# Two blocks of w_in loaded and converted earlier, two first-layer steps moved to attention steps 34 and 35, and four subtractions given to GpSimd

## The chip, the cores and the metric

One core of one Trainium2 chip runs the whole kernel. The metric is the device time of one execution in microseconds (us). Inputs are laid out on the host before the launch, which is not timed.

## What is computed

Three stages follow one another. Attention over q, k, v (4 batches, 8 heads, 576 positions, 64 dimensions) uses a local mask for four heads and a strided mask for the other four. Its output, 2304 tokens by 512, goes through a dense layer pair and then through a routed one:

```
scores = where(mask, q @ k.T / 8, -1e9); attn = softmax(scores); x = attn @ v
h = x @ w_in                       # w_in is 512 x 2048, float64 bits
x2 = (s * relu(h)**2 + b) @ w_out  # w_out is 2048 x 512
logits = x2 @ w_gate               # 8 experts, 288 tokens each, greedy by logit
out[tokens of e] = relu(x2 @ w1[e]) @ w2[e]
```

The arrays `w_in` and `w_out` arrive as 64-bit words and the kernel itself makes float32 from them.

## The kernel before

The kernel is written by hand in a fixed order: each engine runs its own instructions strictly in the order in which the Python code issues them, and waits on semaphores for its operands. Nothing is reordered at run time, so an instruction that waits holds everything behind it on its engine.

**The attention loop.** `mix1` runs a loop over a counter k, called the attention step here. A unit is one pair of heads and one half of the positions of a batch; units 0 to 15 are the first two batches. Unit u starts at step 2u and advances one phase a step. Its phases, with the engine and the line in the kernel before, are:

- step 2u+2: scores on TensorE (L256, L263)
- step 2u+3: row maximum on VectorE (L279, for strided units also the subtraction L290)
- step 2u+4: exponential on ScalarE (L284 or L292)
- step 2u+6: normalisation on VectorE (L296 to L299)
- step 2u+9: transposes on TensorE (L308 or L310)
- step 2u+10: copy of the transposed tile to SBUF on ScalarE (`eT`, L320)
- step 2u+12: product with v on TensorE (L331)
- step 2u+13: copy into `xb` on ScalarE (L336 or L340)

Once enough units are done, `group_x` makes the operands of a group of 384 tokens: a rounded part `xh` on ScalarE (L373) and the rest `xl` on VectorE (L374).

**Blocks of w_in.** `prep(i)` with even i makes block i/2 of the sixteen column blocks of `w_in`. It loads the raw words (L381), takes their absolute value on ScalarE (L406), converts them with four VectorE instructions (L409 to L412), rounds the result to `wh` on ScalarE (L392) and subtracts, `wl = W - wh`, on VectorE (L394). Blocks 0 and 1 go through the pipe `prep0`, which ticks at every second attention step from `P0S` on and starts one block a tick. The later blocks go through `prep`, which ticks at every second step from `P2S = 30` on. A block waits `CA = 4` ticks between the load and the absolute value if `i < 4`, and two ticks otherwise.

**First-layer steps.** `h_step(g, fc)` multiplies group g by block fc on TensorE with twelve matmuls of 128x384: four `wh`·`xh`, four `wh`·`xl` and four `wl`·`xh` (L500), then applies relu and square on ScalarE (L505, L506) and stores the result (L508). `H0` lists the attention steps at which h_step(0, 0) and h_step(0, 1) stand; all other steps follow after the attention loop, the first two of them being (1, 0) and (0, 2). A step's relu is issued when the next step is.

The rest of the program (second layer, routing, experts) is not touched.

Of the kernel before, what the change touches and what calls it, by code (L numbers as in the profile page):

```python
# [13 lines left out]
ALU = mybir.AluOpType  # L14
# [15 lines left out]
def _f(ap):  # L30
    return ap.bitcast(F32)
# [43 lines left out]
class Body:  # L75
# [12 lines left out]
    F2 = 1024  # L88
    WS = 54
    RW = 7  # L90
    CA = 4
    LATE0 = 30
    FA0 = 13
# [8 lines left out]
    A2S = 8  # L102
    TM = 2
    FE = (4, 14, 20)
    P0S = 20
    P2S = 30
    H0 = (36, 38)
    AE = 2
    LOADLAG = 2
    MANUAL = True  # L110
# [39 lines left out]
    def wide(self, shape, dt, s):  # L150
        return self.w.tile(shape, dt, tag="rw", name=self.nm(s), bufs=self.RW)

# [228 lines left out]
        self.nc.sync.dma_start(t.rearrange("p f t -> p (f t)"), self.a["words"][i // 2, i % 2])  # L381
        return t

    def split(self, W, put, wide=False):
        nc = self.nc
        if wide:
            t = self.wide([128, 2, 512], F32R, "wh")
            h, l = t[:, 0], t[:, 1]
        else:
            h = self.wt([128, 512], F32R, "wh")  # L390
            l = self.wt([128, 512], F32R, "wl")
        nc.scalar.copy(h, W)  # L392
        yield
        nc.vector.tensor_tensor(l, W, _f(h), op=ALU.subtract)  # L394
        put((h, l))

    def prep(self, i):

        nc = self.nc
        fc = i // 2  # L400
        raw = self.conv_load(i)
        for _ in range(self.CA if i < 4 or i % 2 else 2):
            yield
        K = self.wt([128, 512], I32, "K")
        ts = nc.vector.tensor_scalar
        nc.scalar.activation(_f(K), _f(raw[:, :, 1]), AF.Abs)  # L406
        yield
        W = self.wt([128, 512], I32, "W")
        ts(_f(K), _f(K), D64_MIN, D64_MAX, op0=ALU.max, op1=ALU.min)  # L409
        ts(K, K, 3, 0x3FFFFFFF, op0=ALU.logical_shift_left, op1=ALU.bitwise_and)  # L410
        nc.vector.scalar_tensor_tensor(W, raw[:, :, 1], -0x40000000, K, op0=ALU.bitwise_and, op1=ALU.bitwise_or)
        nc.vector.scalar_tensor_tensor(K, raw[:, :, 0], 29, W, op0=ALU.logical_shift_right, op1=ALU.bitwise_or)  # L412
        W = _f(K)
        yield
        if i % 2 == 0:
            yield from self.split(W, lambda v: self.win.__setitem__(fc, v))
            return
        nc.sync.dma_start(self.wod[fc], W)
        yield
        yield  # L420
        ps = self.ps()
        for dc in range(4):
            nc.tensor.transpose(ps[:, dc * 128:(dc + 1) * 128], W[:, dc * 128:(dc + 1) * 128], self.identf)  # L423
        yield
        WT = self.wt([128, 512], F32, "WT")
        nc.scalar.copy(WT, ps)
        yield
        self.WTs.append(WT)
        if len(self.WTs) < 4:
            return  # L430
        ps = self.ps()
        for k, WT in enumerate(self.WTs):
            for dc in range(4):
                sl = slice(dc * 128, (dc + 1) * 128)
                nc.tensor.matmul(ps[32 * dc:32 * dc + 32, k * 128:(k + 1) * 128], self.gate[:, dc, :], WT[:, sl],
                                 start=True, stop=True, skip_group_check=True)
        self.WTs.clear()
        yield
        go = self.wt([128, 512], F32, "go")
        nc.scalar.copy(go, ps)  # L440
        yield
        ps = self.ps()
        for k in range(4):
            nc.tensor.transpose(ps[:, k * 128:(k + 1) * 128], go[:, k * 128:(k + 1) * 128], self.identf)
        yield
        nc.vector.tensor_reduce(self.wog[:, fc * 8 - 24:fc * 8 + 8].rearrange("p (f e) -> p f e", e=8),
                                ps.rearrange("p (f c e) -> p f e c", f=4, c=4)[:, :, :8, :], axis=AX.X, op=ALU.add)
        yield
        self.nwog += 4
        if self.nwog == 16:  # L450
            self.prep_end()
# [12 lines left out]
    def load_out(self, fc):  # L464
# [4 lines left out]
        yield  # L469
        yield from self.split(t, lambda v: self.wout.__setitem__(fc, v), fc < self.RW)  # L470
        if fc == 0:
# [117 lines left out]
    def mix1(self):  # L589
# [23 lines left out]
        self.late_pipe = Pipe(self.late_step(g, fc) for g in range(self.NG) for fc in range(16))  # L613
        lead = len(self.H0)
        seq = [(0, fc) for fc in range(lead)] + [(1 - g, fc + g * lead) for fc in range(12) for g in (0, 1)]
# [5 lines left out]
        while self.units < 14 or not self.win or ready:  # L621
            if k in self.H0:
                assert len(self.xg[0]) == 4
# [7 lines left out]
            if self.KS <= k < self.KE:  # L631
                self.keep_warm(self.KW)
            if k >= self.P0S and k % self.P0R == 0:
                prep0.tick()
# [289 lines left out]
    def prep2(self, e, w1, w2):  # L924
        nc, a = self.nc, self.a

        def one(src, put, wide=False):
            t = self.wt([128, 512], F32, "raw2")
            nc.sync.dma_start(t, src)
            yield  # L930
            yield
            yield from self.split(t, put, wide)
# [5 lines left out]
        for fc in range(8):  # L938
            yield one(a["w2"][e, fc * 128:(fc + 1) * 128, :], lambda v, i=fc: w2.__setitem__(i, v),
                      e % 2 == 1 and fc >= 8 - self.RW)  # L940

# [255 lines left out]
```

## Time and profile before

| | us |
|---|---|
| median of 3 runs | 746.08 |
| lowest and highest of these | 744.84, 748.76 |
| the profiled execution, its own time | 750.04 |
| its span from first to last instruction | 748.3 |
| TensorE busy | 724.6 (97%) |
| VectorE busy | 497.0 (66%) |
| ScalarE busy | 371.2 (50%) |
| GpSimd busy | 58.4 (8%) |

The profiled execution took 3.96 us more than the median of the runs. TensorE is busy nearly throughout, and its mean granted clock is 0.987 of full speed. The busy shares are means over stages with different limits, so the stage of the change has to be read by itself.

### The profile page before, as it was taken

To read this page: it belongs to the slowest core of one execution; us is meant where nothing else is said; L and a number is where in the kernel's file an instruction comes from. 1 tells how busy PE (TensorE), PEld (TensorE's weight loads), DVE (VectorE), ACT (ScalarE), POOL (GpSimd) and SP (SyncE) were. 2 spreads that over 40 slices of the span, in tenths; PEclk is the share of its full clock that TensorE was granted. 3 is DMA by queue.
4 is the path that set the end of the run, shared out by engine and by line. 5 is a ranking of instruction groups with operands and counts; after the bars stand their busy time and mean duration, and the time that the engine had idled before them with its cause. 6 is when DMAs were issued, how large, how long until landed. Compare 5 with 4: busy or idle time off the path is not lost.

```text
span 748.3 us, 16505 instructions
## 1 busy us (share of the span) xinstructions
PE 724.6 (97%) x6276; PEld 647.3 (87%) x6276; DVE 497.0 (66%) x1158; ACT 371.2 (50%) x861; POOL 58.4 (8%) x81
## 2 busy tenths in 40 slices
PE   8989999999999999999999998999999999999996
PEld 6769998999999878788778777877999999999994
DVE  6888999986551344378798887785466666666620
ACT  4878775777666555521414221230355554555520
POOL 4000000000000000000000000001102312321211
PEclk9969999999999999999999999999999999999999
DMA  7946866775785899634444423341766676674511
GB/s 232 292 134 201 280 199 198 244 251 191 267 311 187 259 297 288 192 132 144 153 140 143 158 86 116 95 159 44 222 229 180 194 234 202 224 210 146 194 33 32
DMA packets 80047, 140.17 MB, mean 187 GB/s; under 512 B 10336, under 2 KB 43872, under 8 KB 79968
## 3 DMA queue, kind: packets, MB, share of 16 engines
q1 hardware_dynamic: 76896, 129.68, 53.9%
q0 software_dynamic: 3072, 9.44, 3.7%
q8 instruction: 49, 0.80, 0.4%
q14 instruction: 30, 0.25, 0.1%
HBM read 106.32 MB, written 32.77 MB: 186 GB/s over the span
## 4 chain that ended last, share of the span: by engine, by line
PE 85%; DVE 9%; DMA 3%; issue 2%; ACT 0%; POOLq 0%; SPq 0%; DVEq 0%; ACTq 0%
PE b L500 25%; PE b L732 17%; PE b L1000 13%; PE b L1025 11%; PE b L263 3%; PE b L331 2%; PE b L537 2%; DMA r<-ud 2%; PE b L1063 1%; PE b L954 1%; DVE u L704 1%; PE b L1041 1%; PE b L308 1%; DVE E L554 1%; PE b L423 1%
## 5 line engine op out<-in xcount | busy, mean ns | idle before, releaser
L732 PE MATMUL b<-wh,u 128*128 128x512 f32 x663 | 179.6, 391 | 1.1 <-DVE u L704 1.1
L732 PEld LDWEIGHTS b<-wh,u 128*128 128x128 f32 x663 | 121.5, 192 | 17.8 <-DVE u L704 1.8
L701 ACT CAST u<-r 128x384 fp32r<-128x384 f32 (+1 forms) x96 | 46.2, 493 | 130.3 <-DMA r<-ud 62.0
L1025 PE MATMUL b<-u,wh 128*128 128x288 f32 x532 | 90.5, 293 | 0.0
L500 PE MATMUL b<-xh,wh 128*128 128x384 f32 x384 | 84.6, 344 | 0.0
L500 PE MATMUL b<-xh,wl 128*128 128x384 f32 x384 | 79.8, 331 | 2.1 <-DVE wl L394 2.1
L500 PE MATMUL b<-xl,wh 128*128 128x384 f32 x384 | 79.5, 331 | 0.0
L392 ACT CAST wh<-raw 128x512 fp32r<-128x512 f32 x128 | 73.3, 618 | 10.5 <-DVE u L704 10.4
L505 ACT ACTIVATE r<-b 128x384 f32<-128x384 f32 x96 | 46.9, 489 | 63.2 <-PE b L500 61.4
L1025 PEld LDWEIGHTS b<-u,wh 128*128 128x128 f32 x532 | 75.6, 190 | 0.0
L1000 PE MATMUL b<-X,wh 128*128 128x288 f32 x512 | 73.4, 287 | 0.6 <-ACT X L973 0.6
L500 PEld LDWEIGHTS b<-xh,wh 128*128 128x128 f32 x384 | 63.6, 193 | 7.4 <-PE b L537 3.7
L1000 PEld LDWEIGHTS b<-X,wh 128*128 128x128 f32 x512 | 67.4, 189 | 1.3 <-ACT X L973 0.7
L500 PEld LDWEIGHTS b<-xh,wl 128*128 128x128 f32 x384 | 66.0, 192 | 2.9 <-DVE wl L394 2.9
L1007 DVE SCALAR_TENSOR_TENSOR u<-b,u 128x288 fp32r<-128x288 f32 x64 | 29.2, 456 | 57.7 <-ACT u L1006 57.7
L500 PEld LDWEIGHTS b<-xl,wh 128*128 128x128 f32 x384 | 66.2, 192 | 0.0
L394 DVE TENSOR_TENSOR wl<-raw,wh 128x512 fp32r<-128x512 f32 x100 | 65.0, 683 | 0.3
L704 DVE TENSOR_TENSOR u<-r,u 128x384 fp32r<-128x384 f32 (+1 forms) x96 | 47.9, 527 | 17.0 <-ACT u L701 17.0
L732 PE MATMUL b<-wl,u 128*128 128x512 f32 x153 | 58.2, 381 | 0.0
L506 ACT ACTIVATE r<-r 128x384 f32<-128x384 f32 x96 | 50.5, 526 | 3.0
L1006 ACT ACTIVATE u<-b 128x288 fp32r<-128x288 f32 x64 | 26.3, 411 | 50.5 <-PE b L1000 50.2
L1000 PE MATMUL b<-X,wl 128*128 128x288 f32 x256 | 41.9, 286 | 0.0
(209 smaller groups left out, 1096.6 us busy)
## 6 DMA issues: line engine op xcount, KB each, us to landing
raw<-in_moe_w_dram SPq DMA_DIRECT2D x128, 256.0 KB, 4.4
r<-ud SPq DMA_DIRECT2D x160, 192.0 KB, 4.1
ud<-r SPq DMA_DIRECT2D x96, 192.0 KB, 3.0
raw<-in_words_dram SPq DMA_DIRECT2D x32, 512.0 KB, 4.2
qk<-in_q_dram SPq DMA_DIRECT2D x24, 288.0 KB, 4.0
x2d<-E SPq DMA_DIRECT2D x18, 256.0 KB
wod<-K SPq DMA_DIRECT2D x16, 256.0 KB, 2.5
wo<-wod SPq DMA_DIRECT2D x16, 256.0 KB, 4.7
```

The lines of the kernel that those rows point to most:

```text
L392: nc.scalar.copy(h, W)
L394: nc.vector.tensor_tensor(l, W, _f(h), op=ALU.subtract)
L500: nc.tensor.matmul(ps[:, :self.G], w[:, dc * 128:(dc + 1) * 128], _alt(self.xg[g][dc][x]), start=(k == 0), stop=(k == 11))
L505: nc.scalar.activation(_two(r), _nat(ps[:, :self.G]), AF.Relu)
L506: nc.scalar.activation(r, r, AF.Square)
L701: nc.scalar.copy(d[0], src)
L704: nc.vector.tensor_tensor(d[1], src, _f(d[0]), op=ALU.subtract)
L732: self.nc.tensor.matmul(**args)
L1000: self.nc.tensor.matmul(ps[:, :288], w1[dc, fh][wi][:, fs:fs + 128], _alt(X[:, xi, dc, :]), start=(k == 0), stop=(k == 11))
L1006: self.nc.scalar.activation(_two(h), _nat(ps[:, :288]), AF.Relu)
L1007: self.nc.vector.scalar_tensor_tensor(_two(l), _nat(ps[:, :288]), 0.0, _two(_f(h)), op0=ALU.max, op1=ALU.subtract)
L1025: nc.tensor.matmul(y[dc][:, :288], w[:, sl], _alt(u[:, j, :288]), start=(fc == 0 and i == 0), stop=(fc == 7 and i == 2))
```

## The change

Four things change. Blocks 0 and 1 start at attention step 18 rather than 20 (`P0S`), and they wait two ticks rather than four between load and absolute value, as the other blocks do. The steps h_step(0, 0) and h_step(0, 1) stand at attention steps 34 and 35 rather than 36 and 38 (`H0`). The subtraction `wl` of blocks 0 to 3 is issued on GpSimd (`GL = 4`).

```
+    GL = 4
-    P0S = 20
+    P0S = 18
-    H0 = (36, 38)
+    H0 = (34, 35)

-    def split(self, W, put, wide=False):
+    def split(self, W, put, wide=False, by=None):
...
         nc.scalar.copy(h, W)
         yield
-        nc.vector.tensor_tensor(l, W, _f(h), op=ALU.subtract)
+        (by or nc.vector).tensor_tensor(l, W, _f(h), op=ALU.subtract)
...
-        for _ in range(self.CA if i < 4 or i % 2 else 2):
+        for _ in range(self.CA if i % 2 else 2):
             yield
...
-            yield from self.split(W, lambda v: self.win.__setitem__(fc, v))
+            yield from self.split(W, lambda v: self.win.__setitem__(fc, v), by=nc.gpsimd if fc < self.GL else None)
```

Line numbers of the changed kernel are one higher than those of the kernel before from L91 on.

**VectorE, attention steps 24 to 27.** In the kernel before, the normalisation of unit 9 (`E_131`) is followed by the maximum of unit 11, the normalisation of unit 10 (`E_663`) and the maximum of unit 12:

```order
L299 TENSOR_TENSOR E_131<-E_131,nm_613 100x8x36
L279 TENSOR_REDUCE nm_719<-b_694 100x8
L290 TENSOR_TENSOR E_129<-b_694,nm_719 100x8x36
L297 TENSOR_SCALAR nm_662<-nm_662 128x5
L298 RECIPROCAL nm_662<-nm_662 128x5
L299 TENSOR_TENSOR E_663<-E_663,nm_662 128x480
L279 TENSOR_REDUCE nm_766<-b_742 100x8
```

In the changed kernel the same stretch reads:

```order
L300 TENSOR_TENSOR E_131<-E_131,nm_615 100x8x36
L410 TENSOR_SCALAR K_658<-K_658 128x512
L411 TENSOR_SCALAR K_658<-K_658 128x512
L412 SCALAR_TENSOR_TENSOR W_716<-raw_546,K_658 128x512
L413 SCALAR_TENSOR_TENSOR K_658<-raw_546,W_716 128x512
L280 TENSOR_REDUCE nm_728<-b_696 100x8
L291 TENSOR_TENSOR E_129<-b_696,nm_728 100x8x36
L298 TENSOR_SCALAR nm_664<-nm_664 128x5
L299 RECIPROCAL nm_664<-nm_664 128x5
L300 TENSOR_TENSOR E_665<-E_665,nm_664 128x480
L410 TENSOR_SCALAR K_721<-K_721 128x512
```

The four conversion instructions of block 0 (`K_658`) moved ahead of unit 11's maximum and those of block 1 (`K_721`) ahead of unit 12's; before, they stood six steps later, behind the normalisations of units 12 and 13.

**ScalarE, attention steps 34 to 36.** Here stand, before the change, the exponential of unit 15 (`E_965`), `wh` of block 1, the absolute value of block 2, the copies of unit 11 into `xb` and the `eT` copy of unit 13:

```order
L284 ACTIVATE E_965,nm_964<-b_941,nm_964 128x96 x4
L392 CAST wh_1007<-K_896 128x512
L406 ACTIVATE K_1010<-raw_898 128x512
L340 COPY xb_831<-b_979 128x4x36
L340 COPY xb_831<-b_980 128x4x36
L320 COPY eT_1056<-b_1018 96x384
```

And in the changed kernel:

```order
L285 ACTIVATE E_970,nm_969<-b_954,nm_969 128x96 x4
L407 ACTIVATE K_1024<-raw_911 128x512
L506 ACTIVATE r_1028<-b_984 128x384
L507 ACTIVATE r_1028<-r_1028 128x384
L341 COPY xb_850<-b_997 128x4x36
L341 COPY xb_850<-b_998 128x4x36
L321 COPY eT_1073<-b_1048 96x384
```

The rounding of block 1 left this place for an earlier one, and relu and square of h_step(0, 0) moved ahead of unit 11's and unit 13's copies.

**TensorE, attention steps 34 to 36.** Before, the last matmuls of unit 11's product with v (`eT_932`) and the five transposes of unit 13 (`E_838`) stand ahead of the first matmuls of h_step(0, 0):

```order
L331 MATMUL b_980<-eT_932,v_763 64x36 x2
L308 MATMUL b_1018<-identf,E_838 96x128
L308 MATMUL b_1019<-identf,E_838 96x128
L308 MATMUL b_1018<-identf,E_838 96x128
L308 MATMUL b_1019<-identf,E_838 96x128
L308 MATMUL b_1018<-identf,E_838 96x128
L500 MATMUL b_1025<-xh_774,wh_951 128x384
L500 MATMUL b_1025<-xh_778,wh_951 128x384
```

In the changed kernel unit 13's transposes (`E_857`) stand behind the last matmuls of h_step(0, 1):

```order
L501 MATMUL b_1031<-xh_799,wl_848 128x384
L501 MATMUL b_1031<-xh_803,wl_848 128x384
L309 MATMUL b_1048<-identf,E_857 96x128
L309 MATMUL b_1049<-identf,E_857 96x128
L309 MATMUL b_1048<-identf,E_857 96x128
L309 MATMUL b_1049<-identf,E_857 96x128
L309 MATMUL b_1048<-identf,E_857 96x128
L332 MATMUL b_1055<-eT_1015,v_853 64x36 x2
```

h_step(0, 0) now stands directly behind unit 12's transposes, then unit 11's product, then h_step(0, 1), then unit 13's transposes; before, h_step(0, 1) stood behind unit 14's transposes.

## Rows read from the trace of the kernel before

**Rows 1.** Busy time of each engine, stretch by stretch (us from the start).

```profile
core 0: us, PE busy (x) PEld busy (x) DVE busy (x) ACT busy (x) POOL busy (x), PEclk, DMA share, GB/s
30.50:48.20 17.70, 14.16 (x255) 11.47 (x255) 16.80 (x47) 14.46 (x58) 0.00 (x0) 0.84 0.69 223
48.20:54.60 6.40, 6.40 (x50) 5.86 (x51) 6.16 (x13) 5.68 (x16) 0.00 (x0) 0.50 0.16 40
57.40:121.20 63.80, 62.43 (x696) 58.85 (x691) 59.48 (x117) 48.21 (x99) 0.00 (x0) 1.00 0.68 218
```

**Rows 2.** Timeline of TensorE: start, us, instruction, times, idle before and its releaser.

```profile
37.12 0.56 PE L310 MATMUL b<-identf,E 100*128 100x100 f32 x4
...
41.02 0.77 PE L331 MATMUL b<-eT,v 36*64 36x36 f32 x32 [1.03 <-ACT eT L320]
...
48.13 1.65 PE L500 MATMUL b<-xh,wl 128*128 128x384 f32 x4 [1.01 <-DVE wl L394]
```

**Rows 3.** The same busy view, microsecond by microsecond, where the granted clock changes.

```profile
42.00:43.00 1.00, 0.00 (x0) 0.00 (x0) 0.93 (x4) 1.00 (x8) 0.00 (x0) 0.74 0.60 242
...
56.00:57.00 1.00, 1.00 (x22) 0.88 (x18) 0.00 (x0) 0.33 (x2) 0.00 (x0) 0.93 0.13 49
```

**Rows 4.** The chain that ended last, in order of time: first-layer matmuls.

```profile
51.82 3.84 PE b L500 x12
57.81 4.10 PE b L500 x24
```

**Rows 5.** Timeline of VectorE around the conversions of blocks 0 and 1.

```profile
36.17 0.46 DVE L299 TENSOR_TENSOR E<-E,nm 100x288 f32<-100x288 f32 x1
...
38.61 0.42 DVE L409 TENSOR_SCALAR K<-K 128x512 f32<-128x512 f32 x1
...
40.25 0.69 DVE L412 SCALAR_TENSOR_TENSOR K<-raw,W 128x512 int32<-128x512 int32 x1
...
57.38 0.63 DVE L374 TENSOR_TENSOR xl<-xb,xh 128x192 fp32r<-128x192 f32 x2 [2.77 <-ACT xh L373]
```

**Rows 6.** Landing of the raw words in the first 60 us: count, size, median us.

```profile
raw<-in_words_dram SPq DMA_DIRECT2D x8, 512.0 KB, 6.4
```

**Rows 7.** Timeline of ScalarE from unit 13's copy to the operands of h_step(1, 0).

```profile
48.89 0.80 ACT L320 COPY eT<-b 96x384 f32<-96x384 f32 x2
49.57 0.71 ACT L406 ACTIVATE K<-raw 128x512 f32<-128x512 f32 x1
...
50.83 0.66 ACT L340 COPY xb<-b 128x144 f32<-128x144 f32 x2 [0.55 <-PE b L331]
...
51.28 0.61 ACT L373 CAST xh<-xb 128x192 fp32r<-128x192 f32 x2
...
52.74 0.62 ACT L320 COPY eT<-b 96x256 f32<-96x256 f32 x2
...
53.78 0.68 ACT L406 ACTIVATE K<-raw 128x512 f32<-128x512 f32 x1
...
56.67 0.42 ACT L336 COPY xb<-b 128x320 f32<-128x320 f32 x1 [2.22 <-PE b L331]
57.00 0.60 ACT L373 CAST xh<-xb 128x192 fp32r<-128x192 f32 x2
```

**Rows 8.** Timeline at 120 us: subtractions of two later blocks and the matmuls behind them.

```profile
120.54 1.29 DVE L394 TENSOR_TENSOR wl<-K,wh 128x512 fp32r<-128x512 f32 x2
...
121.28 0.92 PE L500 MATMUL b<-xh,wl 128*128 128x384 f32 x4 [1.06 <-DVE wl L394]
```

**Rows 9.** Timeline of GpSimd in the first 10 us.

```profile
2.11 3.93 POOL L188 TENSOR_SCALAR_AFFINE_SELECT mloc<-mloc 64x96 bf16<-64x96 bf16 x8
...
7.95 0.52 POOL L198 MEMSET z<- 128x512 f32 x1
8.43 0.37 POOL L627 IOTA R<- 128x144 f32 x1
```

**Rows 10.** Timeline of VectorE in the first 11 us: one operation twice.

```profile
8.43 0.40 DVE L297 TENSOR_SCALAR nm<-nm 100x8 f32<-100x8 f32 x1
...
10.72 0.17 DVE L297 TENSOR_SCALAR nm<-nm 100x8 f32<-100x8 f32 x1
```

## The prediction, made before the changed kernel was run

> **What bounds the kernel now.** I read the busy time by stretches first. In the attention loop, from 30.5 to 48.2 us, VectorE is busy for 16.80 of 17.70 us, which with the gaps between instructions is full; TensorE is busy for 14.16 us, much of it short matmuls [rows 1]. So VectorE sets the pace there. From 48.2 to 54.6 us VectorE is still nearly full, and TensorE is busy throughout but at a granted clock of 0.50, its lower level of 1.2 GHz [rows 1]. From 57.4 to 121.2 us TensorE is busy for 62.43 of 63.80 us at full clock (2.4 GHz), and VectorE for 59.48: both are close to full, and the reader should not take only one for the bound [rows 1].
>
> The timeline of TensorE says where it stopped: 1.03 us before unit 11's product at 41.02 us and 1.01 us before the `wl` matmuls of h_step(0, 0) at 48.13 us [rows 2]. Between 42 and 43 us TensorE does nothing and the clock falls to its lower level; it is back in the microsecond from 56 us on [rows 3]. What the lower clock costs is seen in the chain of waits: twelve first-layer matmuls take 3.84 us at 51.82 us, and twenty-four take 4.10 us at 57.81 us, so twelve take 2.05 us; one block at the lower clock costs 1.8 us more [rows 4]. The rise came after h_step(0, 1) had run its twelve matmuls without a pause, to 55.66 us.
>
> **The change, part by part.**
>
> *Conversions of blocks 0 and 1.* One conversion runs from 38.61 to 40.94 us, 2.33 us [rows 5]. The work is the same as before, but both conversions now stand ahead of unit 11's normalisation, where nothing of them stood before. VectorE has no free time to put them in from 30.5 us on [rows 1], so everything behind slides by 2 x 2.33 = 4.66 us. Unit 11's normalisation ended at 36.17 + 0.46 = 36.63 us [rows 5] and will end at about 41.3 us. Unit 11's transposes, at 37.12 us before [rows 2], start at 41.4 us, and TensorE waits some 4 us in all, in place of the stops that it had. That is longer than the stops after which the clock fell, so I take the lower clock here too.
>
> *The two first-layer steps.* Between the start of unit 11's transposes and the end of unit 12's, where h_step(0, 0) now stands, lie 2.87 us of TensorE work: 37.12 to 41.02 - 1.03 = 39.99 us [rows 2]. From 41.4 us this brings h_step(0, 0) to 44.3 us at full clock and to 47.1 us at half; I take 47.1, since the idle time stands right ahead. All its operands are there, so the stop of 1.01 us is gone. At the lower clock it takes 3.84 us, to 51.0 us. By the pattern of before the clock rises after this undisturbed block, 5 us sooner than it did. Then come unit 11's product (0.77 us) [rows 2], h_step(0, 1) (2.05 us) and unit 13's five transposes (0.7 us, from 0.56 for four [rows 2]): 54.5 us.
>
> *What is queued behind.* ScalarE's copy of unit 13's transposes ran at 48.89 us [rows 7]. It now waits for transposes that stand behind both first-layer steps, until 54.5 us, and holds the whole ScalarE queue. Behind it, to the last `xh` that h_step(1, 0) needs, lie four pieces: 48.89 to 50.28, 50.83 to 51.89, 52.74 to 54.46 and 56.67 to 57.60 us, that is 1.39 + 1.06 + 1.72 + 0.93 = 5.10 us [rows 7]. So `xh` is complete at 59.6 rather than 57.60 us, and h_step(1, 0) starts at 59.8 rather than 57.81 us: 2.0 us late. ScalarE's idle time of 2.22 us ahead of 56.67 us [rows 7], which covered a later queue before, is used up by this.
>
> *The subtractions.* VectorE loses two `wl` of blocks 2 and 3 behind this point, 1.29 us by the row of two such subtractions [rows 8]. For blocks 0 and 1 the same amount falls away too late to help the chain above. GpSimd has no `tensor_tensor` in this trace. The bounds of its cost are 0.52 us, a memset of the same shape that reads nothing, and 2.6 us, the affine_select's 3.93 / 8 = 0.49 us for 96 elements scaled to 512 [rows 9]; an iota of 144 elements in 0.37 us [rows 9] scales to 1.3 us. I take 1.2 us, nearest to the last. By itself this is hidden at any of these values: block 0's subtraction has from about 35 to 47 us, and those of blocks 2 and 3 are read by steps that stand a whole block of matmuls or more later. Whether it also slows VectorE is the third rival.
>
> *Loads.* The raw words land in 6.4 us [rows 6] and are now needed four steps after their place instead of eight. SP runs ahead of the engines and the other blocks keep the same distance, so I cost this at nothing; at worst it is part of the 6.4 us once, on ScalarE, before 30 us.
>
> *The sum.* At 121.28 us TensorE waits 1.06 us for a `wl` of VectorE [rows 8]. TensorE arrives 2.0 us later, so 2.0 - 1.06 = 0.9 us are left of it; VectorE arrives 2.0 - 1.29 = 0.7 us later. The later one decides: 0.9 us. One cost may come on top. TensorE has some 3 us of attention work after 54.5 us, and then stands until 59.8 us for nearly 2 us. If the clock falls there again and rises after one block, that is 1.8 us more: 2.7 us. I see no row that settles it, and forecast the middle, +1.8 us. The rest of the program follows unchanged. The profiled execution would go from 750.04 to 751.8 us. It lies 3.96 us above the median of the runs, so I put the difference on the median: 746.08 + 1.8 = 747.9 us.
>
> **The rivals.**
>
> *Faster.* The conversions find free time. Units 9 and 10 may run a little sooner, because the words load earlier, and VectorE may then begin the conversions before 30.5 us. If TensorE keeps its clock and unit 13's copy on ScalarE isn't late, that queue is only changed by relu and square in front (1.0 us) less one rounding (0.6 us): `xh` is complete at 48.89 + 0.4 + 5.10 = 54.4 us, 3.2 us early, and the 1.06 us at 121 us is gained too [rows 7, 8]: -4.3 us, 741.8 us. For it speak the gaps that the two early steps fill, and the lower clock from 42 to 56 us; against it, VectorE without free time [rows 1]. It decides from the point at which unit 13's transposes end by 49 us.
>
> *No more than a reshuffle.* The clock does not fall before h_step(1, 0): +0.9 us, 747.0 us. With the clock falling again it is 748.8 us. Both are within 0.5% of before, which is about what a measurement of this kernel can tell from no change.
>
> *Slower: GpSimd holds VectorE.* At 8.43 us a VectorE operation on 8 columns takes 0.40 us, while the same one takes 0.17 us at 10.72 us [rows 10]; GpSimd's iota runs from 8.43 to 8.80 us, almost exactly the long one's time [rows 9]. If VectorE's operations wait like this for each subtraction, two of them stand ahead of unit 11's normalisation, and the chain is later by 2 x 1.2 = 2.4 us (1.0 to 5.2 by the bounds): +3.3 to +5.1 us, 750.3 us in the middle. It passes 0.5% from a subtraction of about 0.95 us on. Against it: one row, and VectorE's reductions beside a memset show nothing.
>
> The Trainium skill, "SBUF — State Buffer", section "SBUF: two separate sides", has this as a rule: VectorE and GpSimd share a pair of SBUF ports under an exclusive lock, which a VectorE instruction with two SBUF inputs or in a two-port mode needs, so that one blocks the other fully. The row at 8.43 us agrees with it. By the Trainium skill's "GPSIMD Engine Reference", section "3.1 Elementwise — side-by-side cycle accounting", 2048 elements of a tensor_tensor take 4497 ns; a quarter, 1.1 us, would be an estimate here, and two holds would then cost 2.2 us. No run so far shows that duration.
>
> **How the numbers follow.** I give +0.9 us (no second fall) 0.30, +2.7 us (second fall) 0.28, the hold 0.24, the faster case 0.16, and 0.02 to none of these. The forecast, 747.9 us, lies between the first two, whose own range is 746 to 749.5 us. The range of 742.0 to 751.5 us leaves out the better half of the faster case and the upper part of the hold, under 0.2 together. Slower by over 0.5% (above 749.8 us) is most of the hold and the upper tail of the second fall: 0.26. Faster (below 742.3 us) is 0.16, and the rest, 0.58, lies within 0.5%.
>
> **What would show it.** In the profile after, unit 11's transposes should start near 41 us behind a wait for VectorE; h_step(0, 0) should run its twelve matmuls without a stop; unit 13's copy should wait for TensorE until about 54 us; h_step(1, 0) should start near 60 us behind a wait for ScalarE; the wait at 121 us should be gone. The hold would show as VectorE instructions longer than before exactly beside GpSimd's subtractions. The prediction is wrong if VectorE takes up the conversions without delaying unit 11, or if the clock never falls, or if GpSimd's subtraction costs far more than 1.3 us.

## The result, and the profile after

The changed kernel is slower: 753.9 us median over 9 runs (751.07 to 756.89), against 748.58 us for the kernel before, run 9 times beside it (744.84 to 750.48). The ratio is 1.0083, 95% interval 1.0062 to 1.0104; applied to 748.58 us that is +6.2 us. The forecast was +1.8 us. It was set on a median of 746.08 us from three runs; the nine runs put the kernel before 2.5 us higher, so the two medians are compared here by their ratio. The profiled execution of after took 756.89 us by its own time, span 755.1 us; the one of before had 750.04 and 748.3 us. Both lie above their medians, after's by 3.0 us, so single positions in these two traces are good to some 3 us.

Busy time by stretches, before first, then after; the columns are those of [rows 1].

```profile
20.00:30.00 10.00, 9.74 (x242) 7.62 (x242) 7.51 (x22) 7.89 (x37) 0.00 (x0) 1.00 0.99 300
30.00:42.00 12.00, 10.76 (x267) 8.55 (x261) 11.38 (x31) 10.18 (x42) 0.00 (x0) 1.00 0.99 313
42.00:57.00 15.00, 12.70 (x89) 11.09 (x89) 12.06 (x30) 10.78 (x39) 0.00 (x0) 0.54 0.20 69
57.00:70.00 13.00, 13.00 (x104) 12.51 (x103) 11.21 (x21) 11.41 (x25) 0.00 (x0) 1.00 0.53 178
```

```profile
20.00:30.00 10.00, 7.18 (x180) 5.76 (x180) 5.43 (x16) 6.64 (x30) 0.00 (x0) 0.93 0.87 262
30.00:42.00 12.00, 10.28 (x224) 8.13 (x222) 9.69 (x22) 7.14 (x25) 1.40 (x1) 0.91 0.74 227
42.00:57.00 15.00, 12.34 (x121) 10.46 (x121) 13.38 (x37) 10.81 (x46) 1.93 (x1) 0.66 0.39 128
57.00:70.00 13.00, 11.16 (x104) 9.39 (x102) 10.03 (x17) 8.57 (x23) 2.54 (x2) 0.74 0.33 102
```

The reader is to see two things. Already in the first stretch, where the change was expected to do nothing, TensorE works 7.18 us instead of 9.74 and VectorE 5.43 instead of 7.51. And in the last, where the clock of before was full, the mean granted clock of after is 0.74. TensorE's timeline of after shows the places (start, us, instruction, times, idle before and its releaser):

```profile
28.00 0.26 PE L264 MATMUL b<-qk 64*36 64x36 f32 x4 [2.81 <-issue]
...
46.61 0.90 PE L311 MATMUL b<-identf,E 100*128 100x100 f32 x4 [1.90 <-DVE E L300]
...
51.24 1.55 PE L501 MATMUL b<-xh,wh 128*128 128x384 f32 x4
52.63 0.81 PE L501 MATMUL b<-xl,wh 128*128 128x384 f32 x4
...
56.68 0.71 PE L309 MATMUL b<-identf,E 128*96 128x128 f32 x5
...
62.24 0.79 PE L501 MATMUL b<-xh,wh 128*128 128x384 f32 x3 [1.03 <-ACT xh L374]
...
64.02 1.33 PE L501 MATMUL b<-xl,wh 128*128 128x384 f32 x3 [0.67 <-DVE xl L375]
...
129.40 0.92 PE L501 MATMUL b<-xh,wl 128*128 128x384 f32 x4 [1.06 <-DVE wl L395]
```

The first row is new in size: TensorE stops for 2.81 us between the 28th and the 29th of the 32 score matmuls of unit 9, and waits for nothing that the profile shows. Before, the same place had this row:

```profile
25.49 0.26 PE L263 MATMUL b<-qk 64*36 64x36 f32 x4 [0.26 <-issue]
```

Then unit 11's transposes, 9.5 us later than in [rows 2]; h_step(0, 0) without a stop, the clock rising inside it (its first four matmuls take 1.55 us, the next four 0.81); unit 13's transposes behind both first-layer steps; and h_step(1, 0), stopped twice. The stop that stood at 121.28 us [rows 8] stands at 129.40 us, 8.1 us later and as long as before: 1.06 us. By the end of the program 1.3 of these 8.1 us are given back (755.1 - 748.3 = 6.8).

VectorE's normalisation of unit 9 stood here before:

```profile
30.08 0.46 DVE L299 TENSOR_TENSOR E<-E,nm 100x288 f32<-100x288 f32 x1
```

VectorE of after, around unit 9's and 11's normalisations and the conversions:

```profile
28.31 0.46 DVE L280 TENSOR_REDUCE nm<-b 100x8 f32<-100x288 f32 x1 [3.37 <-PE b L264]
...
34.08 0.46 DVE L300 TENSOR_TENSOR E<-E,nm 100x288 f32<-100x288 f32 x1
...
34.91 0.43 DVE L411 TENSOR_SCALAR K<-K 128x512 int32<-128x512 int32 x1
...
39.01 1.38 DVE L411 TENSOR_SCALAR K<-K 128x512 int32<-128x512 int32 x1
...
44.98 0.75 DVE L298 TENSOR_SCALAR nm<-nm 100x8 f32<-100x8 f32 x1
...
46.00 0.46 DVE L300 TENSOR_TENSOR E<-E,nm 100x288 f32<-100x288 f32 x1
...
60.94 1.74 DVE L412 SCALAR_TENSOR_TENSOR W<-raw,K 128x512 int32<-128x512 int32 x1
...
64.33 1.48 DVE L411 TENSOR_SCALAR K<-K 128x512 int32<-128x512 int32 x1
```

GpSimd's four subtractions in the same trace (its spans are rough):

```profile
38.71 1.40 POOL L395 TENSOR_TENSOR wl<-K,wh 128x512 fp32r<-128x512 f32 x1 [29.91 <-DVE E L300]
43.77 1.93 POOL L395 TENSOR_TENSOR wl<-K,wh 128x512 fp32r<-128x512 f32 x1 [3.66 <-ACT wh L393]
60.83 1.27 POOL L395 TENSOR_TENSOR wl<-K,wh 128x512 fp32r<-128x512 f32 x1 [15.12 <-ACT wh L393]
64.25 1.27 POOL L395 TENSOR_TENSOR wl<-K,wh 128x512 fp32r<-128x512 f32 x1 [2.16 <-ACT wh L393]
```

Beside each stands one long VectorE instruction: 1.38 for 0.43 us, 0.75 for 0.17 (the short one of [rows 10]), 1.74 for about 0.7, 1.48 for 0.43, 3.6 us together. The first two are ahead of unit 11's normalisation (46.00 us); unit 9's stands at 34.08 us.

The chain of before had this at the place of the stop (start, us, piece):

```profile
25.23 0.26 issue
```

The chain of after has two long pieces there and at h_step(1, 0):

```profile
25.19 2.81 issue
...
64.02 6.11 PE b L501 x19
```

Nineteen such matmuls take 19 x 0.171 = 3.25 us at full clock by [rows 4]; here the clock had fallen again, to 0.50 from 63 to 69 us, and they cost 2.9 us more.

### The profile page after: what moved, and what is told of

Same layout as the page of the kernel before. It is cut to its first block, busy times and chain, and to the rows that moved or that the text cites. A ratio compares the mean times of both kernels' runs of the same rounds, so it can differ in the third digit from the quotient of the medians.

```text
span 755.1 us, 16514 instructions
## 1 busy us (share of the span) xinstructions
PE 726.0 (96%) x6276; PEld 648.1 (86%) x6276; DVE 498.1 (66%) x1154; ACT 370.6 (49%) x861; POOL 63.9 (8%) x85
## 4 chain that ended last, share of the span: by engine, by line
PE 81%; DVE 12%; DMA 3%; issue 2%; ACT 1%; SPq 0%; POOLq 0%; DVEq 0%; ACTq 0%
PE b L501 23%; PE b L733 16%; PE b L1001 13%; PE b L1026 11%; PE b L264 3%; PE b L538 2%; PE b L332 2%; DMA r<-ud 2%; PE b L1064 1%; PE b L955 1%; DVE u L705 1%; PE b L1042 1%; DVE E L555 1%; PE b L424 1%; PE b L989 1%
```

## The experiments

Twelve kernels were run, each beside the kernel before. Three theories were to be told apart. **Order** (theory A in the expectations): conversions and steps at other places. **Hold** (theory B): GpSimd's subtractions make VectorE's instructions wait. **Loads** (theory C): the raw words, loaded at steps 18 and 20, lengthen TensorE's stop in unit 9's scores. e1 to e5 take the parts of the change alone or out, e6 and e7 vary the transfers, and e8 to e12 the places that were left.

| kernel | loads at steps | conversions | first-layer steps | subtracts | median | ratio to before, 95% |
|---|---|---|---|---|---|---|
| the change | 18, 20 | early | 34, 35 | GpSimd | 753.9 | 1.0083 (1.0062–1.0104) |
| e1 | 18, 20 | early | 34, 35 | VectorE | 750.45 | 1.0020 (0.9994–1.0046) |
| e2 | 18, 20 | as before | 36, 38 | VectorE | 750.38 | 1.0031 (1.0010–1.0051) |
| e3 | 20, 22 | early | 34, 35 | GpSimd | 750.34 | 1.0031 (1.0012–1.0051) |
| e4 | 20, 22 | as before | 36, 38 | GpSimd | 747.7 | 0.9994 (0.9974–1.0013) |
| e5 | 20, 22 | early | 34, 35 | VectorE | 748.48 | 1.0001 (0.9977–1.0024) |
| e6 | 12, 14 | as before | 36, 38 | VectorE | 748.39 | 1.0005 (0.9982–1.0029) |
| e7 | 20, 22, and more | as before | 36, 38 | VectorE | 750.92 | 1.0042 (1.0020–1.0064) |
| e8 | 10, 12 | steps 16, 18 | 36, 38 | VectorE | 745.75 | 0.9967 (0.9947–0.9987) |
| e9 | 10, 12 | steps 16, 18 | 34, 35 | VectorE | 745.08 | 0.9948 (0.9930–0.9965) |
| e10 | 10, 12 | steps 16, 18 | 36, 38 | GpSimd | 745.39 | 0.9949 (0.9931–0.9967) |
| e11 | 20, 22 | early | 36, 38 | VectorE | 747.44 | 0.9975 (0.9959–0.9991) |
| e12 | 12, 14 | early | 34, 35 | GpSimd | 751.8 | 1.0038 (1.0018–1.0057) |

"Early" is where the change has them. The kernel before had medians of 748.3 to 748.7 us beside these runs.

**e1, the change with VectorE's subtractions.** `GL = 4` becomes `GL = 0`.

> The changed kernel with all subtractions on VectorE again. Theory A (the conversions stand ahead of units 11 and 12, and two first-layer steps ahead of unit 13's transposes): most of the loss stays, ratio 1.005 to 1.007 to the kernel before. Theory B (GpSimd's subtractions hold VectorE, some 1 us each): about 3 us come back, ratio 1.003 to 1.005, and the VectorE instructions of 1.38, 0.75, 1.74 and 1.48 us are back at 0.43, 0.17, 0.7 and 0.43 us. Theory C (loads two steps earlier delay TensorE's own instructions): the wait of 2.8 us at 28 us stays and h_step(1, 0) is still late.

1.0020, and no long VectorE instruction is left. VectorE and TensorE of e1 at unit 11's normalisation:

```profile
40.87 0.17 DVE L298 TENSOR_SCALAR nm<-nm 100x8 f32<-100x8 f32 x1
...
41.69 0.69 DVE L395 TENSOR_TENSOR wl<-K,wh 128x512 fp32r<-128x512 f32 x1
```

```profile
26.33 0.26 PE L264 MATMUL b<-qk 64*36 64x36 f32 x4 [0.81 <-issue]
...
41.92 0.90 PE L311 MATMUL b<-identf,E 100*128 100x100 f32 x4 [2.14 <-DVE E L300]
```

VectorE's own subtraction of block 0 stands behind unit 11's normalisation. GpSimd's run ahead of it, at 38.71 and 43.77 us in after, and the time for which they hold VectorE falls there. The hold is real: the intervals of e1 and of the change don't meet. The load theory expected the stop of 2.8 us to stay; with the same loads it is 0.81 us here, so its size in after does not follow from the place of the loads alone.

**e2, the kernel before with only the loads at steps 18 and 20** (block 0 and 1 then wait five ticks, so that the conversions keep their place).

```
-    P0S = 20
+    P0S = 18
-        for _ in range(self.CA if i < 4 or i % 2 else 2):
+        for _ in range(5 if i < 4 and i % 2 == 0 else self.CA if i % 2 else 2):
```

> The kernel before with only the two loads of raw words moved, from attention steps 20 and 22 to 18 and 20; the conversions, the first-layer steps and the subtractions stay. Theory C: TensorE's wait inside unit 9's scores grows from 0.26 us to about 2.8 us, and the time grows by 2 to 4 us, ratio 1.003 to 1.005. Theories A and B: no change, ratio 1.000, and the wait stays near 0.3 us.

1.0031. The stop in unit 9's scores is 1.28 us:

```profile
26.40 0.26 PE L263 MATMUL b<-qk 64*36 64x36 f32 x4 [1.28 <-issue]
```

The `wl` matmuls of h_step(0, 0) start at 49.20 us, 1.07 us later than in [rows 2], as much as the stop has grown. The wait ahead of them is 2.98 rather than 1.01 us because TensorE arrives sooner: its clock falls only at 49 us here, and before at 42. The loads alone cost something.

**e3, the change with the loads back at steps 20 and 22** (`P0S = 20`, one tick of waiting).

> The changed kernel with the two loads back at attention steps 20 and 22 and everything else as changed (one tick between load and absolute value). Theory C: the wait at 28 us shrinks to about 0.3 us, and 2.5 to 4 us come back, ratio 1.003 to 1.005. Theory A and B: the loss stays, ratio 1.007 to 1.009. If the words land too late for one tick, ScalarE waits for them before the absolute value, up to 2 us.

1.0031, no stop in unit 9's scores, and the long VectorE instructions are all there:

```profile
34.91 1.38 DVE L411 TENSOR_SCALAR K<-K 128x512 int32<-128x512 int32 x1
...
40.86 0.75 DVE L298 TENSOR_SCALAR nm<-nm 100x8 f32<-100x8 f32 x1
```

**e4, the kernel before with GpSimd's subtractions alone** (`GL = 4` and the `by` argument).

> The kernel before with only the four subtractions given to GpSimd. Theory B: each subtraction takes 1.3 to 1.9 us and lengthens one or two VectorE instructions beside it by about 1 us, and the wl matmuls of h_step(0, 0) come later, since GpSimd takes longer than VectorE's 0.68 us; ratio 1.001 to 1.004. Theory A alone: no loss from this part, ratio 0.998 to 1.001, since VectorE has 2.7 us less to do.

0.9994. Four VectorE instructions are long here as well (1.64, 1.33, 1.74 and 1.74 us), but the time is even: VectorE has four subtractions less, TensorE no longer waits 1.01 us for `wl`, and in this trace the clock is full again from 46 us on, before from 57. A hold need not cost by itself; that what stands behind it decides is argued from the places, not tested alone.

**e5, the change with late loads and VectorE's subtractions**, so only the conversions and the steps moved.

> The changed kernel without two of its parts: loads back at steps 20 and 22, all subtractions on VectorE. What is left is the earlier conversion of blocks 0 and 1 and the two first-layer steps at 34 and 35. If the parts add (the load part cost about 0.5% and the GpSimd part about 0.6% of the changed kernel), ratio 0.997 to 0.999 to the kernel before. Theory A (the order by itself costs 1 to 3 us): ratio 1.001 to 1.004. In both, no wait of over 0.5 us inside unit 9's scores and no VectorE conversion instruction over 1 us before 60 us.

1.0001. The order by itself is even, within some 0.2% either way. TensorE of e5:

```profile
41.05 0.90 PE L311 MATMUL b<-identf,E 100*128 100x100 f32 x4 [2.13 <-DVE E L300]
...
45.67 0.90 PE L501 MATMUL b<-xh,wh 128*128 128x384 f32 x4
46.40 0.81 PE L501 MATMUL b<-xl,wh 128*128 128x384 f32 x4
47.05 0.81 PE L501 MATMUL b<-xh,wl 128*128 128x384 f32 x4
...
50.45 0.71 PE L309 MATMUL b<-identf,E 128*96 128x128 f32 x5
...
56.00 0.76 PE L501 MATMUL b<-xh,wh 128*128 128x384 f32 x3 [1.02 <-ACT xh L374]
```

**e6, the kernel before with the loads far ahead** (`P0S = 12`, eight ticks), **and e7, the kernel before with four loads more** of 256 KB, two each at steps 17 and 19, whose data nothing reads:

```
+            if k in (17, 19):
+                for j in range(2):
+                    x = self.wt([128, 512], I32, "x")
+                    nc.sync.dma_start(x, self.a["words"][0, 0][:, 512 * j:512 * j + 512])
```

> The kernel before with the two loads far ahead, at attention steps 12 and 14 instead of 20 and 22, and everything else in its place. Theory C as a collision (TensorE's own instructions are fetched at about 25 us over the same DMA engines, and the loads at steps 18 and 20 lie right ahead of that): no wait inside unit 9's scores beyond 0.3 us, ratio 0.998 to 1.001. Theory C as mere earliness: the wait is 1 to 3 us, ratio 1.003 or more. Waits for qk or v may appear earlier, near 15 us.

> The kernel before with additional transfers and nothing else: two of 256 KB after attention step 17 and two after step 19, of words that no instruction reads. The loads of blocks 0 and 1 keep their place. Theory C as a collision: the wait inside unit 9's scores grows to 1 to 3 us or more, and the time by 2 to 4 us, ratio 1.002 to 1.006. If the fetch has nothing to do with the loads: wait 0 to 0.3 us, ratio 0.999 to 1.001.

e6 is even (1.0005) and has no stop; e7 is slower (1.0042), its stop is 1.54 us, and the clock falls behind it as in after (0.50 from 28 to 31 us). So it isn't that the loads come sooner, but that they come there.

**e8, all of it far ahead**: the kernel before with `P0S = 10` and two ticks, so that the conversions come eight steps ahead of the change's.

> A version that could beat both: the kernel before with blocks 0 and 1 loaded at attention steps 10 and 12 and converted at steps 16 and 18, where VectorE has some free time, subtractions on VectorE, first-layer steps at 36 and 38 as before. If free time takes up the 4.7 us of conversions: unit 11 is not late, the stops of TensorE at 41 to 48 us shrink, and the time falls by 2 to 5 us, ratio 0.993 to 0.998. If the earlier loads hold up the loads of q, k and v, or the conversions displace units 5 to 8 instead: ratio 0.999 to 1.005, with waits of TensorE before 35 us.

0.9967, better than both kernels. Why is seen with e9.

**e9, e8 with the steps at 34 and 35; e10, e8 with GpSimd's subtractions; e11, e5 with the steps at 36 and 38; e12, the change with the loads at steps 12 and 14** (`P0S = 12`, five ticks).

> Blocks 0 and 1 load at steps 10 and 12, VectorE subtracts, and the two first-layer steps stand at 34 and 35. If the step order is what cost the time (order theory), this is slower than the same kernel with the steps at 36 and 38 (ratio 0.997) by 0.4% or more, 1.001 or above. If the order is even, and the loads and the hold of VectorE by GpSimd are the costs, it is 0.995 to 0.999, and no instruction packet for TensorE begins after 23.5 us with a stop behind it.

> Blocks 0 and 1 load at steps 10 and 12, the steps stand at 36 and 38 as before, and GpSimd subtracts for blocks 0 to 3. Hold theory: VectorE instructions beside a subtraction are about 1 us longer, four in all; where VectorE sets the pace this costs 2 to 4 us against the same kernel with VectorE's subtractions (ratio 0.997), so 1.000 to 1.002. If the hold costs only in company with the early loads, it stays at 0.996 to 0.998.

> Only the conversions of blocks 0 and 1 move ahead (loads at steps 20 and 22, steps at 36 and 38, VectorE subtracts). Order theory, with the conversions as the delay of unit 11: slower by 0.3% or more (1.003). If conversions and steps are even by themselves: 0.998 to 1.002, unit 11's transposes at about 41 us as in the version with the steps at 34 and 35.

> The change with only the two loads put far ahead, to steps 12 and 14; conversions, step order and GpSimd's subtractions as in the change. Load theory (the loads at steps 18 and 20 delay TensorE's instruction packets): no stop in unit 9's scores, the packet at 23.2 us or sooner, and the ratio that of the change with late loads, 1.003 (1.001 to 1.005), against 1.008 for the change. If it is not the place of the loads but the hold and the order alone: 1.008 again.

e12 is what the load theory said: 1.0038 against 1.0083 for the change, with everything but the loads the same, and both holds ahead of unit 11 (1.38 and 0.75 us). The 32 score matmuls of unit 9 run without a stop:

```profile
24.67 0.75 PE L264 MATMUL b<-qk 64*36 64x36 f32 x32
```

Its transposes of unit 11 come at 42.27 us.

e11 is 0.9975, and its interval leaves out 1: the conversions alone, moved ahead on a nearly full VectorE, gained some 0.25% where the order theory expected a loss. In its trace TensorE has no stop of 0.2 us or more between unit 11's transposes at 41.57 us and 110 us; in e5 it stops once more, at 56.00 us.

The expectation for e10 was missed: 0.9949, though a cost of 2 to 4 us was expected. Two VectorE instructions are 1 us longer in it and a pair of them 0.5 us; but beside one subtraction next to nothing happens. GpSimd and VectorE of e10 there:

```profile
29.07 1.27 POOL L395 TENSOR_TENSOR wl<-K,wh 128x512 fp32r<-128x512 f32 x1 [2.47 <-ACT wh L393]
```

```profile
29.29 0.46 DVE L291 TENSOR_TENSOR E<-b,nm 100x288 f32<-100x288 f32 x1
29.67 0.44 DVE L297 TENSOR_REDUCE nm<-E 100x8 f32<-100x288 f32 x1
30.14 0.23 DVE L298 TENSOR_SCALAR nm<-nm 100x8 f32<-100x8 f32 x1
```

The reduction and the `tensor_tensor` that reads a score tile `b` from PSUM take their usual time; the `tensor_scalar` is held for 0.06 us, to 30.37 us, where the subtraction ends (30.34). All four holds sum to about 2.5 us, and VectorE is spared four subtractions of 0.69 us, 2.8 us: even.

e9 is the fastest, 0.9948 (e10 is level with it), and its spread is 744.82 to 745.87 us over 6 runs, where before had 744.68 to 751.31 over 23. The stretches of e9, as above:

```profile
20.00:30.00 10.00, 9.35 (x222) 7.23 (x221) 9.52 (x24) 8.43 (x35) 0.00 (x0) 1.00 0.74 209
30.00:42.00 12.00, 10.22 (x239) 8.07 (x239) 11.39 (x32) 8.97 (x39) 0.00 (x0) 1.00 0.93 306
42.00:57.00 15.00, 13.11 (x162) 11.25 (x162) 12.73 (x33) 14.94 (x52) 0.00 (x0) 1.00 0.23 82
```

VectorE takes up the conversions between 20 and 30 us, where it had 2.5 us free (9.52 busy, 7.51 before), and TensorE keeps its full clock through 42 to 57 us, where before had 0.54. In e10 the clock is down for some 3 us of this stretch (0.50 from 45 to 48 us), and the time is the same. The granted clock goes with the time in the kernel before too. Of its 93 executions beside the experiments the seven whose mean granted clock is 0.995 or 0.996 took 744.2 to 745.3 us, as little as e9 (0.994 to 0.998), and those at 0.987 took 747.6 to 751.3 us. So e9 seems to gain mostly by keeping the clock up every time. Between 34, 35 and 36, 38 the intervals overlap in both pairs (e8 and e9, e11 and e5), with opposite signs: the runs don't tell them apart.

**What lies behind the stop.** The queue list of the trace (queue, packets, MB, share) shows single 16 KB packets of a queue named instruction, each within the half microsecond quoted: before at 22.5, after at 25.0, e12 at 22.0 us.

```profile
q8 instruction: 1, 0.02, 17.0%
```

```profile
q8 instruction: 1, 0.02, 15.2%
```

```profile
q8 instruction: 1, 0.02, 16.6%
```

In slices of 0.1 us, this packet begins at 21.5 to 23.4 us in every kernel that has no load of raw words at steps 17 to 19 (before 22.6, e3 22.8, e5 23.1, e11 23.4), at 23.8 to 23.9 in e1, e2 and e7, and at 25.2 in after. Where TensorE stops, the 29th matmul starts 2.4 to 2.9 us after it: before 25.49 - 22.6 = 2.9, e1 2.4, e2 2.6, e5 2.4, e7 2.5, after 28.00 - 25.2 = 2.8 us. Where the packet began 2.7 us or more ahead of the 29th matmul's turn (e3: 24.89 + 0.68 - 22.8 = 2.8 us; e12: 24.67 + 0.68 - 22.0 = 3.4 us), there is no stop. The trace doesn't say which engine a packet serves, but the counts of a whole execution do point to one. The row of the engines and this queue's row of after (before has the same counts for TensorE and the queue):

```profile
PE 726.0 (96%) x6276; PEld 648.1 (86%) x6276; DVE 498.1 (66%) x1154; ACT 370.6 (49%) x861; POOL 63.9 (8%) x85
```

```profile
q8 instruction: 49, 0.80, 0.5%
```

The 2 x 6276 matmuls and weight loads make 256 for each of the 49 packets; the other engines of this row have fewer than 24 a packet. So the packet very likely carries TensorE's next instructions. That it is late because the 16 DMA engines, 99% busy from 20 to 30 us before, are taken by data, fits all of this and is argued.

## Why the prediction was wrong, step by step

**Loads: the step that failed.** "I cost this at nothing" rested on when the words land and how far SP runs ahead. What the transfers push aside was not asked. The change against e12 puts the place of the loads at 1.0083 - 1.0038 = 0.45%, and against e3 at 0.52%: 3.4 to 3.9 of the 6.2 us. That is their price with the hold in place. Without the hold it is smaller: 0.31% in e2, and 0.19%, within the noise, between e1 and e5. In the profiled execution unit 9's normalisation came at 34.08 rather than 30.08 us, 4.0 us, of which the longer stop is 2.81 - 0.26 = 2.55 us. The rest goes with the clock, which fell behind the stop and was at its lower level from 30 to 32 us, as the row of after shows:

```profile
30.00:32.00 2.00, 2.00 (x22) 1.55 (x21) 0.52 (x2) 0.60 (x2) 0.00 (x0) 0.50 0.50 188
```

**Subtractions: the price was about right, "hidden by itself" was not.** GpSimd took 1.27 to 1.93 us, where 1.2 was taken. The estimate of 1.1 us from the Trainium skill, "GPSIMD Engine Reference", section "3.1 Elementwise — side-by-side cycle accounting", lies below the least of these. The hold, given 0.24 as a rival, is what happened beside the loads: VectorE longer exactly beside the subtractions. Of the change, e3 and e12 (1.0031, 1.0038) against e5 (1.0001) put it at 0.30 to 0.37%, 2.3 to 2.8 us, though each interval alone overlaps e5's; the rival's sum said 2.4 us for two holds ahead of unit 11. With the early loads in place, the change against e1, it is 0.63%, 4.7 us. In the trace the two holds ahead of unit 11 are 0.95 + 0.58 = 1.5 us, and unit 11's transposes are 1.2 to 1.4 us later in e12 and e3 than in e5; the later holds, at blocks 2 and 3, stand ahead of h_step(1, 0)'s second stop. The rule of the Trainium skill, "SBUF — State Buffer", section "SBUF: two separate sides", that a VectorE instruction with two SBUF inputs or in a two-port mode is blocked fully while GpSimd has the shared ports, agrees with the row at 44.98 us, which ends at 45.73 as the subtraction ends at 45.70 (the trace doesn't show its mode), and with e10, where the reduction and the PSUM reader pass.

**Conversions: right.** Unit 11's transposes were put at 41.4 us; with neither loads nor hold (e5) they came at 41.05, behind a wait for VectorE. In after the two costs above, 4.0 and 1.5 us, came on top: 46.61 us.

**First-layer steps and the clock: right order, wrong size.** h_step(0, 0) ran without a stop. But the clock did not wait for its end. In e5 the granted clock is 0.67 between 45 and 46 us and full from 46 us on, so it came back as the block began; its twelve matmuls run from 45.67 to 47.86 us, 2.19 us where 3.84 were taken. Unit 13's transposes end at 50.45 + 0.71 = 51.16 us (54.5 predicted) and h_step(1, 0) is past its `xh` wait at 56.00 (59.8 predicted, 57.81 before). In after, too, the block takes less than was taken, 2.55 us by the chain, since the clock rose inside it. So the queue of ScalarE, though it waits for TensorE as said, was not by itself what made the change slow: without loads and hold, h_step(1, 0) is 1.8 us early rather than 2.0 us late.

**The wait at 121 us: wrong.** It was to take up 1.06 us of a delay. In all fourteen traces it is 1.04 to 1.06 us, wherever TensorE arrives, so the two sides move together, and it has no slack to give. Why is only hinted at: the chain of before leads back from this wait, through VectorE's queue and a load of `v`, to ScalarE's relu of a block of TensorE itself at 110.71 us.

**The second clock fall** was left open between 0.9 and 2.7 us. It came in after, between h_step(1, 0)'s two stops, and cost 2.9 us there (19 matmuls in 6.11 us). It did not come in the traces of e1, e3, e5 or e12, which have the same two stops or one of them. It isn't that one traced execution alone: the mean granted clock, on record for every execution, is over the whole program 0.983 to 0.989 in the nine of the change, 0.986 on average, against averages of 0.990 for e1 and e3, 0.989 for e2 and e12, and 0.989 to 0.990 for before. So TensorE is longer at its lower level in the change than with either the loads or the hold taken out. This fits that the parts don't add (0.20 for e1, which has the loads, and 0.31 for e3, which has the hold, against 0.83%). By its ratio either part alone would have left the time within the stated range of 742.0 to 751.5 us (747.6 and 748.4 us on 746.08). What decides whether the clock falls there stays open.

## What to carry to other kernels

A transfer that is moved has a price where it lands, even if its data is early: look at which stretch has the DMA engines full, and whether TensorE there stops on "issue" inside a run of equal matmuls. Giving VectorE's element-wise work to GpSimd moves its time to wherever VectorE runs beside it, so look at what stands behind it there. Work on an engine that is full is best moved into a stretch where it has idle time, as e9 does: the same conversions and steps, with the loads and the conversions eight steps sooner and the subtractions left on VectorE, gain 0.5% (0.35 to 0.70%) where the change lost 0.8%. And read the granted clock of every execution, not only of the traced one.

## What the runs showed of the hardware

TensorE's stop inside unit 9's scores was 0.26 us before and 0.81 to 2.81 us in the four kernels with more transfers just ahead of it (e1, e2, e7, after). In all six traces that show it, it ended 2.4 to 2.9 us after the start of one 16 KB packet of an instruction queue, of which there is one for every 256 TensorE instructions. GpSimd's subtraction of 128 x 512 took 1.27 us at the least, and 1.93 us beside VectorE work, which itself waited (0.75 for 0.17 us): both lose. The clock came back from its lower level inside h_step(0, 0) in after (1.55 us for four matmuls, then 0.81) and as it began in e5; before, it had stayed low through both first-layer steps.
